# Windowed attention and two float64-weight feed-forward layers on one core: the sign of the weights carried by ScalarE's parametric ReLU, and the order of the work found anew

## The chip, the cores and the metric

The kernel runs on one core of one Trainium2 chip. The metric is the device time of one execution in microseconds (us), as the median of several runs. A profiled execution shows where that time goes: TensorE (PE, with its weight loads as PEld), VectorE (DVE), ScalarE (ACT), GpSimd (POOL) and the DMA queue that SyncE (SP) issues.

## The reference, cut to what matters

Attention over 4 batches, 8 heads, 576 positions and head size 64 (heads 0 to 3 see the last 32 positions, heads 4 to 7 every fourth of the last 128) gives x of 2304 x 512. Two feed-forward layers follow:

```python
def _moe_ref(x, w_in, w_out) -> np.ndarray:       # w_in 512 x 2048, w_out 2048 x 512
    h = x @ w_in
    g = h * np.cos(h)
    return (g @ w_out).astype(np.float32)
...
def _moe2_ref(x, w_gate, w_val, w_out) -> np.ndarray:   # 512 x 1536 twice, 1536 x 512
    gate = 1.0 / (1.0 + np.exp(-(x @ w_gate)))
    val = x @ w_val
    return (gate * val @ w_out).astype(np.float32)
...
        out['moe_' + k] = m[k]
```

The five weight matrices are float64 (a float32 draw times a Python float scale). The chip reads each as pairs of 32-bit words, and the kernel makes float32 values of them itself.

## The kernel before, in words

**The work.** Attention is done in units of 192 positions and half of the heads. The first layer goes over six chunks of 384 tokens. It takes 96 steps: `mlp_tasks(n)` multiplies one chunk with one block of 128 columns of w_in (`mm_h`, 12 matmuls into `ps_h`), makes h * cos(h) on ACT and DVE (`turn`, `part`, `cosine`, `g`, `g_hi`, `g_lo`) and multiplies with one block of w_out (`mm_x2`, 12 matmuls into four `acc` tiles). Steps 0 to 47 use the first eight column blocks for all six chunks, and the attention of later chunks runs beside them. Steps 48 to 95 use the other eight blocks. At the end of a chunk's eight steps, `take` (in `x2_out`) empties the four `acc` tiles, in the second half by an addition on DVE; the next chunk's first `mm_x2` needs those banks. The second layer follows, with pairs of chunks and seven products in place of eight.

**The weights.** 68 of the weight tiles of 128 x 512 values go through `w_tasks(i)`. Each is loaded as words (`raw`, printed as `wst`: the even words are the low halves of the doubles, the odd words the high halves). `low` (ACT) moves the low words down by 29 bits. `mag` reads the high word as a float32 and multiplies by 2^-112, which corrects the exponent; it stands on ACT, or on DVE where the scheduler finds DVE free first (`alt`). `shift` (DVE) moves the result up by three bits, which pushes the sign out. `top` (DVE) puts the sign back by taking the top bit of the high word. `rnd` (DVE) adds the low words. `hi` and `lo` split the value into two parts for TensorE, `lo` and the like on POOL.

**The order.** Nothing is ordered by hand. `Plan` is a scheduler that runs while the kernel is built: every task has an engine, a duration in a table, predecessors, buffers that it takes and gives back, and a priority. The task names are those of `add(("w_mag", i), ...)`. The priority is a place in the program plus a number by name from `NUDGE`, for priorities under `NUDGE_UNTIL`. Every instruction of every engine's queue and of SP's comes out in the order that this run gives. A task with `port=True` is kept apart in the plan from others that use the same port. Where PE would be idle in the plan before step 7, `keep_warm` fills in matmuls of a 128 x 128 identity (`identb`); their number comes from the plan.

Of the kernel before, what the change touches and what calls it, by code (L numbers as in the profile page):

```python
# [9 lines left out]
F32 = mybir.dt.float32  # L10
# [4 lines left out]
AF = mybir.ActivationFunctionType  # L15
ALU = mybir.AluOpType
# [20 lines left out]
X2_LAG = 3.5  # L37
SEC = 2.75
W_PRIO, W_START = 4.5, -4
W_GATE = (12.0, 1.8, 36.0, 1.4, 70.0, 1.6)  # L40
W_PRE = (6.0, 1.3)
W_MIX = (2, 2)
PRE = (0, 2, 4, 6)
O_START, O_PACE, O_LEAD = 2.5, 1.05, 2.0
XS_LEAD = (15.0, 0.6)
QK_LEAD, V_LEAD = 2, 3.0
A_LEAD, EXP_LEAD = 2.1875, 0.5
COLD, DENSE = 1.25, 1.0
NUDGE_UNTIL = 16
NUDGE = {"head": 4.5, "k_out": 0.75, "load_qk": -0.75, "load_v": 3.75, "p_out": -2, "p_transp": -2.5, "pv": -3.75,  # L50
         "q_out": -0.5, "s_eps": 2.75, "s_exp": 1, "s_max": -1, "s_norm": -1.25, "s_rec": 3.5, "scores": -4.5, "transp": -0.25,
         "w_hi": -0.25, "w_load": 0.5, "w_mag": 2, "w_rnd": -0.5, "x": -10.25, "x_hi": -3.75, "x_save": -8.5}
WARM, WARM_NS = 1200, 57


class Plan:
# [28 lines left out]
    def add(self, key, eng, dur, fn, deps=(), prio=0.0, take=(), give=(), table=None, port=False, lat=None, step=None,  # L85
            after=(), gate=None, alt=None, dma=0):
        assert key not in self.tasks, key
        if prio < NUDGE_UNTIL:
            prio += NUDGE.get(key[0], 0.0)
        self.tasks[key] = dict(key=key, eng=eng, dur=dur, fn=fn, deps=deps, prio=prio, take=take, give=give, table=table,  # L90
                               port=port, lat=lat or 0, step=step, after=after, gate=gate, alt=alt, dma=dma)

# [136 lines left out]
def windowed_attention_mlp_kernel(ctx, tc, q, k, v, w_in, w_out, w_gate, w_val, w_out2, out):  # L229
# [12 lines left out]
    PE, ACT, DVE, POOL, SP = nc.tensor, nc.scalar, nc.vector, nc.gpsimd, nc.sync  # L242
# [20 lines left out]
    scale = 1.0 / float(D) ** 0.5  # L263
# [41 lines left out]
    late = {}  # L305
# [12 lines left out]
    add = plan.add  # L318
# [48 lines left out]
    def pos(g):  # L367

        if g < 0:
            return NEG_GS * g  # L370
        c = min(int(g / GPC), NC - 1)
        return begin[c] + (g / GPC - c) * FIRST[c]
# [19 lines left out]
    def w_tasks(i):  # L392
        key = kind, f = wseq[i]
        st = {}
        j = i - 2 * F1
        if i in w_pre:
            need = W_PRE[0] + (w_order.index(i) - 2 * CUT) * W_PRE[1] + 14
        elif i < 2 * CUT:
# [3 lines left out]
        elif kind == "out2":  # L402
            need = W_GATE[4] + (j - 2 * F2) * W_GATE[5] + 8
        else:
            need = NSTEP + SEC * f
        pr = need - W_PRIO + i * 1e-3
        pre = 0 <= j < 2 * F2 and f in PRE
        block = j >= 0 and not pre
        second = kind == "val" or kind == "out2" and f % 2 == 1
        wid = (kind == "out2", f // 2 if kind == "out2" else f)  # L410
        nw = j // 2
# [10 lines left out]
            t = st["raw"][:, :, 0]  # L422
            ACT.activation(out=t, in_=t.bitcast(U32), func=AF.Copy, scale=2.0**-29)  # L423

        def mag(on_dve=False):

            st["c"] = wst.tile([P, DM], I32, tag="wc", name="wc")
            c, x = st["c"].bitcast(F32), st["raw"][:, :, 1].bitcast(F32)
            if on_dve:
                DVE.tensor_scalar(c, x, 2.0**-112, None, op0=ALU.mult)  # L430
            else:
                ACT.activation(out=c, in_=x, func=AF.Copy, scale=2.0**-112)

        def shift():
            DVE.tensor_scalar(st["c"], st["c"], 3, None, op0=ALU.logical_shift_left)

        def top():
            DVE.scalar_tensor_tensor(st["c"], st["raw"][:, :, 1], -0x80000000, st["c"], op0=ALU.bitwise_and,
                                     op1=ALU.bitwise_or)

        def rnd():
            to = st["c"]
# [18 lines left out]
        elif j < 0 or pre:  # L461
            gate = W_PRE[0] + (w_order.index(i) - 2 * CUT) * W_PRE[1]
        else:
            gate = need - 8 if kind == "out2" else min(W_GATE[2] + j * W_GATE[3], need - 8)
        add(("w_load", i), "sp", 550, load, [], pr - 2 if i >= 2 * FIRST[0] else max(NEG_GS * (i / 4 - 6) + W_START, pos(-A_LEAD - 1) - QK_LEAD + 0.1), take=["raw"], dma=1900, gate=gate,
            after=[("w_load", w_order[w_order.index(i) - 1])] if i else [])
        add(("w_low", i), "act", 520, low, [("w_load", i)], pr)

        def keep():
# [3 lines left out]
        def again():  # L473
            SP.dma_start(out=lf(TB_AT[nw % 2], 2 * DM), in_=wf2[PRE.index(f)])

        add(("w_mag", i), "act", 550, mag, [("w_load", i)], pr, take=["wc"], alt=("dve", 335, lambda: mag(True), True))
        add(("w_shift", i), "dve", 335, shift, [("w_mag", i)], pr, port=True)
        add(("w_top", i), "dve", 600, top, [("w_shift", i)], pr, port=True)
        give = ["raw"] + (["wc"] if block else [])
        deps = [("w_top", i), ("w_low", i)] + (["late"] if block else []) + ([] if not block else [("w_rnd", i - 1)] if second else [("w_free", nw - 2)] if nw >= 2 else [])  # L480
        add(("w_rnd", i), "dve", 600, rnd, deps, pr, give=give, port=True)
        if pre:
            add(("w_keep", i), "sp", 450, keep, [("w_rnd", i)], pr, give=["wc"], dma=800)
            if second:
                pr = NSTEP + SEC * f - W_PRIO + i * 1e-3
                add(("w_again", nw), "sp", 450, again, [("w_keep", i - 1), ("w_keep", i), "late"] + ([("w_free", nw - 2)] if nw >= 2 else []),
                    pr - 2, dma=1200, gate=min(W_GATE[2] + j * W_GATE[3], NSTEP + SEC * f - 8))
                block_tasks(i, nw, wid, pr, [("w_again", nw)])
# [449 lines left out]
    def p2(n):  # L938
        return NSTEP + SEC * n

    def xs_tasks(s):
# [7 lines left out]
        for kk in range(2):  # L949
# [20 lines left out]

            base = p2(s * F2) - XS_LEAD[0] + kk * 7 * XS_LEAD[1]
            gate = base - 1.0
# [19 lines left out]
            for i, nm in enumerate(("a0", "s2", "a1", "s3", "s1", "b1", "s4")):  # L992
                pr = base + i * XS_LEAD[1]
                deps = src[nm] + [("x2", early, KD - 1)]
# [7 lines left out]
    def xs_wide(s, ca, cb):  # L1002
# [19 lines left out]

        base = p2(s * F2) - XS_LEAD[0]
        free = w_saved if s == 1 else [("o_save", s - 2, nm, i) for nm in ("A0", "A1", "B0", "B1") for i in range(TT)]
# [372 lines left out]
```

## Time and profile before

| | |
|---|---|
| median of 3 runs | 936.86 us (934.87 to 937.38) |
| profiled execution | 940.28 us, of which its span, first to last instruction, is 938.5 us |
| PE busy | 922.5 us, 98% of the span |
| DVE busy | 721.5 us, 77% |
| ACT busy | 491.4 us, 52% |
| POOL busy | 190.3 us, 20% |
| granted TensorE clock, mean | 0.994 |

A matmul is counted as busy from its start to its modelled end, so a busy PE can still start its matmuls at a larger distance than it could. Busy shares are means over stages that differ.

### The profile page before, as it was taken

The page shows a single profiled execution, that of the slowest core. Times are in us where ns is not written, and L with a number is a line of the kernel's source. Part 1 is how long each engine was busy: PE and PEld are TensorE (multiplying, and loading weights), DVE is VectorE, ACT ScalarE, POOL GpSimd, SP SyncE. Part 2 cuts the span into 40 slices and gives each one's busy share as a digit, 9 for nine tenths or more (in the row PEclk, how much of TensorE's full clock was granted, in tenths as well). Part 3 has the DMA queues.
Part 4 walks back from the last instruction along what each step waited for, and adds up shares of the span by engine and source line. Part 5 has one row for each costly group of instructions (what it writes and reads, how often), then busy time and mean ns, then how long its engine had stood idle before and what let it go on. Part 6 is the DMA issues. An engine that isn't in the chain of part 4 may idle for free.

```text
span 938.5 us, 19283 instructions
## 1 busy us (share of the span) xinstructions
PE 922.5 (98%) x6921; PEld 897.6 (96%) x6921; DVE 721.5 (77%) x1726; ACT 491.4 (52%) x1182; POOL 190.3 (20%) x208
## 2 busy tenths in 40 slices
PE   8999999999999999999989999999999999999998
PEld 7898989989999999999989999999999999999998
DVE  5898898878977878898989865775666786566683
ACT  5787868767776655555556622342333343332261
POOL 4444322232313444323242400000000000000000
PEclk9999999999999999999989999999999999999999
DMA  7976757576335799879877698877888987887693
GB/s 190 210 219 164 209 163 217 148 220 173 95 116 184 249 357 312 308 246 301 307 244 276 221 378 278 302 233 252 267 269 268 324 297 251 267 267 214 191 324 107
DMA packets 162639, 225.67 MB, mean 240 GB/s; under 512 B 60784, under 2 KB 127088, under 8 KB 161520
## 3 DMA queue, kind: packets, MB, share of 16 engines
q1 hardware_dynamic: 161744, 224.24, 74.6%
q8 instruction: 55, 0.90, 0.4%
q14 instruction: 40, 0.33, 0.1%
q10 hardware_dynamic: 800, 0.20, 0.1%
HBM read 168.82 MB, written 55.57 MB: 239 GB/s over the span
## 4 chain that ended last, share of the span: by engine, by line
PE 74%; DVE 11%; DMA 9%; issue 3%; ACT 3%; SPq 0%; ACTq 0%; DVEq 0%
PE acc L775 5%; PE ps_h L775 5%; PE ps_h L777 4%; PE ps_h L776 4%; PE acc L777 4%; PE acc L776 4%; PE ps_y L1082 4%; PE ps_y L1084 4%; PE ps_y L1083 4%; PE xy L1230 3%; DMA wst<-in_moe_w_out_dram 3%; PE xy L1232 3%; PE xy L1231 3%; PE ps_x L1082 3%; PE ps_x L1084 3%
## 5 line engine op out<-in xcount | busy, mean ns | idle before, releaser
L520 POOL TENSOR_TENSOR lr<-lf,lr 128x512 fp32r<-128x512 f32 (+1 forms) x72 | 92.1, 1297 | 170.1 <-ACT lr L516 137.0
L775 PE MATMUL acc<-gs,arena 128*128 128x384 f32 x240 | 85.0, 354 | 0.4 <-ACT o L911 0.3
L777 PE MATMUL acc<-gs,arena 128*128 128x384 f32 x240 | 80.7, 336 | 0.0
L776 PE MATMUL acc<-gs,arena 128*128 128x384 f32 x240 | 80.5, 335 | 0.0
L845 DVE TENSOR_TENSOR gs<-u,gs 128x384 fp32r<-128x384 f32 x96 | 68.5, 715 | 11.8 <-ACT gs L842 11.4
L1082 PE MATMUL ps_y<-arena 128*128 128x384 f32 x216 | 73.1, 338 | 0.2 <-DVE u L1100 0.2
L1084 PE MATMUL ps_y<-arena 128*128 128x384 f32 x216 | 72.4, 335 | 0.0
L1083 PE MATMUL ps_y<-arena 128*128 128x384 f32 x216 | 72.3, 335 | 0.0
L825 ACT ACTIVATE r<-ps_h 128x384 int32<-128x384 f32 x96 | 46.7, 486 | 48.7 <-PE ps_h L777 48.1
L832 ACT ACTIVATE u<-u 128x384 f32<-128x384 f32 x96 | 50.0, 523 | 39.3 <-DVE u L829 38.3
L775 PE MATMUL ps_h<-arena 128*128 128x384 f32 x192 | 68.6, 357 | 0.6 <-DVE arena L718 0.6
L835 DVE TENSOR_TENSOR u<-ps_h,u 128x384 f32<-128x384 f32 x96 | 52.8, 552 | 17.0 <-ACT u L832 16.4
L777 PE MATMUL ps_h<-arena,wb 128*128 128x384 f32 x192 | 65.1, 339 | 0.0
L776 PE MATMUL ps_h<-arena,wb 128*128 128x384 f32 x192 | 65.1, 339 | 0.0
L775 PE MATMUL ps_h<-arena,wb 128*128 128x384 f32 x192 | 65.1, 339 | 0.0
L777 PE MATMUL ps_h<-arena 128*128 128x384 f32 x192 | 64.5, 336 | 0.0
L776 PE MATMUL ps_h<-arena 128*128 128x384 f32 x192 | 64.4, 335 | 0.0
L829 DVE SCALAR_TENSOR_TENSOR u<-ps_h,r 128x384 f32<-128x384 f32 x96 | 52.9, 551 | 13.7 <-ACT r L825 13.4
L1115 ACT ACTIVATE sg<-sg 128x384 f32<-128x384 f32 x36 | 19.0, 527 | 83.7 <-DVE sg L1111 83.7
L674 ACT ACTIVATE s<-s,mx 128x80 f32<-128x80 f32 (+1 forms) x168 | 59.3, 358 | 0.1
L423 ACT ACTIVATE wst<-wst 128x512 int32<-128x512 uint32 x68 | 45.5, 672 | 24.0 <-DMA wst<-in_moe_w_in_dram 10.5
L775 PE MATMUL acc<-gs,wb 128*128 128x384 f32 x144 | 49.3, 343 | 4.2 <-DVE o L905 3.2
(201 smaller groups left out, 2948.3 us busy)
## 6 DMA issues: line engine op xcount, KB each, us to landing
arena<-wd SPq DMA_DIRECT2D x108, 512.0 KB, 4.7
lr<-od SPq DMA_DIRECT2D x42, 512.0 KB, 4.8
wd<-lr SPq DMA_DIRECT2D x36, 512.0 KB, 4.8
wst<-in_moe_w_out_dram SPq DMA_DIRECT2D x28, 512.0 KB, 4.7
arena<-od SPq DMA_DIRECT2D x21, 512.0 KB, 6.1
arena<-wd SPq DMA_DIRECT2D x36, 256.0 KB, 3.9
od<-lr SPq DMA_DIRECT2D x18, 512.0 KB, 4.7
wst<-in_moe_w_in_dram SPq DMA_DIRECT2D x16, 512.0 KB, 5.5
```

The lines of the kernel that those rows point to most:

```text
L520: POOL.tensor_tensor(out=l, in0=x, in1=h.bitcast(F32), op=ALU.subtract)
L674: ACT.activation(out=s, in_=s, func=AF.Exp, scale=-1.0, bias=row("mx", u)[:, i:i + 1], accum_out=row("rs", u)[:, i:i + 1])
L775: PE.matmul(ps, wh, xl, start=first, stop=False)
L776: PE.matmul(ps, wl, xh, start=False, stop=False)
L777: PE.matmul(ps, wh, xh, start=False, stop=last)
L829: DVE.scalar_tensor_tensor(st["u"], st["h"], INV_2PI, st["r"], op0=ALU.mult, op1=ALU.subtract)
L832: ACT.activation(out=st["u"], in_=st["u"], func=AF.Sin, scale=TWO_PI, bias=HALF_PI)
L835: DVE.tensor_tensor(out=st["u"], in0=st["h"], in1=st["u"], op=ALU.mult)
L845: DVE.tensor_tensor(out=st["gs"][:, 1, :], in0=st["u"], in1=st["gs"][:, 0, :].bitcast(F32), op=ALU.subtract)
L1082: PE.matmul(st[to], wh, xl, start=first, stop=False, **more)
L1083: PE.matmul(st[to], wl, xh, start=False, stop=False, **more)
L1084: PE.matmul(st[to], wh, xh, start=False, stop=kk == 1, **more)
```

## The change

`mag` uses the activation function Prelu in place of Copy, with the same factor 2^-112 and the slope 2^32 for negative values. A negative value so comes out with an exponent field that is larger by 32, and `shift` by three bits moves exactly that bit into the place of the sign, while the old sign bit falls out at the top. `top` is then not needed, and `rnd` waits for `shift`. `mag` stands on ACT alone; the form on DVE is gone. The numbers that set the order are others: four of the pacing constants change, `NUDGE` has new numbers, and two more tables, `NUDGE_MID` and `NUDGE_LATE`, reach the tasks with larger priorities, which had no such numbers.

```diff
-W_GATE = (12.0, 1.8, 36.0, 1.4, 70.0, 1.6)
-W_PRE = (6.0, 1.3)
+W_GATE = (13.0, 1.8, 36.0, 1.2, 70.0, 1.6)
+W_PRE = (6.0, 1.38)
...
-O_START, O_PACE, O_LEAD = 2.5, 1.05, 2.0
-XS_LEAD = (15.0, 0.6)
-QK_LEAD, V_LEAD = 2, 3.0
+O_START, O_PACE, O_LEAD = 2.2, 1.05, 1.2
+XS_LEAD = (15.0, 0.7)
+QK_LEAD, V_LEAD = 2.3, 3.0
...
-NUDGE_UNTIL = 16
-NUDGE = {"head": 4.5, "k_out": 0.75, "load_qk": -0.75, "load_v": 3.75, "p_out": -2, "p_transp": -2.5, "pv": -3.75,
...
+NUDGE_UNTIL, NUDGE_FROM = 16, 44
+NUDGE = {"k_out": -1.25, "load_qk": 0.5, "load_v": 2.5, "p_out": -4.5, "pv": -3.75, "s_eps": 2.25, "s_exp": 1,
...
+NUDGE_LATE = {"o_hi": -3.5, "o_lo": -3, "o_sum": -7.5, "w2": -0.25, "w2_save": -3.5, "w_again": 8.25, "w_blo": -2.75,
...
-        if prio < NUDGE_UNTIL:
-            prio += NUDGE.get(key[0], 0.0)
+        if key[0] != "warm":
+            prio += (NUDGE if prio < NUDGE_UNTIL else NUDGE_MID if prio < NUDGE_FROM else NUDGE_LATE).get(key[0], 0.0)
...
-        def mag(on_dve=False):
+        def mag():
 
             st["c"] = wst.tile([P, DM], I32, tag="wc", name="wc")
-            c, x = st["c"].bitcast(F32), st["raw"][:, :, 1].bitcast(F32)
-            if on_dve:
-                DVE.tensor_scalar(c, x, 2.0**-112, None, op0=ALU.mult)
-            else:
-                ACT.activation(out=c, in_=x, func=AF.Copy, scale=2.0**-112)
+            ACT.activation(out=st["c"].bitcast(F32), in_=st["raw"][:, :, 1].bitcast(F32), func=AF.Prelu, scale=2.0**-112,
+                           alpha=2.0**32)
 
         def shift():
             DVE.tensor_scalar(st["c"], st["c"], 3, None, op0=ALU.logical_shift_left)
 
-        def top():
-            DVE.scalar_tensor_tensor(st["c"], st["raw"][:, :, 1], -0x80000000, st["c"], op0=ALU.bitwise_and,
-                                     op1=ALU.bitwise_or)
-
...
-        add(("w_mag", i), "act", 550, mag, [("w_load", i)], pr, take=["wc"], alt=("dve", 335, lambda: mag(True), True))
+        add(("w_mag", i), "act", 550, mag, [("w_load", i)], pr, take=["wc"])
         add(("w_shift", i), "dve", 335, shift, [("w_mag", i)], pr, port=True)
-        add(("w_top", i), "dve", 600, top, [("w_shift", i)], pr, port=True)
...
-        deps = [("w_top", i), ("w_low", i)] + (["late"] if block else []) + ([] if not block else [("w_rnd", i - 1)] if second else [("w_free", nw - 2)] if nw >= 2 else [])
+        deps = [("w_shift", i), ("w_low", i)] + (["late"] if block else []) + ([] if not block else [("w_rnd", i - 1)] if second else [("w_free", nw - 2)] if nw >= 2 else [])
```

The line numbers of the changed kernel are larger by six up to `low` and smaller by two from the block tasks on; between them `mag` is `L434` (`L432`), `shift` is `L438` (`L435`; the `L438` of before is `top`), `rnd` is `L445` (`L446`) and `hi` on ACT is `L452` (`L453`).

In the whole program as built, PE has the same matmuls but for the fillers: 267 on `identb` before, 286 now. DVE has 1728 instructions before and 1633 now, ACT 1018 and 1045; 34 of the 68 `mag` stood on ACT before, 68 do now. In the first 48 steps of the first layer 18 `mag` stood on ACT and 44 do now. PE's matmuls of scores and of values (`ps_s`, `ps_v`) stand in 54 unbroken groups before and in 51 now. Loads of an activation table: 21 before, 21 now.

**ACT at the start of the program.** `qbp` and `ktp` are the copies of the first transposed q and k (`ps_t`) that the first attention scores wait for, `wst` and `wc` are the weight tiles (`low`, `mag`), `s,rs` the exponentials. Before:

```order
L642 ACT_TABLE_LOAD
L642 ACTIVATE qbp<-ps_t 128x192
L423 ACTIVATE wst<-wst 128x512
L642 ACTIVATE ktp<-ps_t 128x192
L423 ACTIVATE wst<-wst 128x512
L432 ACTIVATE wc<-wst 128x512
L674 ACTIVATE s,rs<-s,mx 128x96 x2
```

Now:

```order
L640 ACT_TABLE_LOAD
L640 ACTIVATE ktp<-ps_t 128x192
L434 ACTIVATE wc<-wst 128x512
L429 ACTIVATE wst<-wst 128x512
L434 ACTIVATE wc<-wst 128x512
L452 ACTIVATE arena<-wc 128x512
L672 ACTIVATE s,rs<-s,mx 128x96 x2
```

Before, the second copy on ACT stood behind a weight tile; now the one copy that ACT makes stands ahead of all weights.

**DVE at the start of the program**, the first rows behind the clearing of buffers. Before:

```order
L646 COPY ktp<-ps_t 128x192
L430 TENSOR_SCALAR wc<-wst 128x512
L646 COPY qbp<-ps_t 128x192
L435 TENSOR_SCALAR wc<-wc 128x512
L438 SCALAR_TENSOR_TENSOR wc<-wst,wc 128x512
```

Now:

```order
L644 COPY qbp<-ps_t 128x192
L644 COPY ktp<-ps_t 128x192
L644 COPY qbp<-ps_t 128x192
L438 TENSOR_SCALAR wc<-wc 128x512
L445 ISA wc<-wst,wc 128x1024
```

Three of the four copies stand on DVE now, all ahead of the first weight work.

**DVE where the chunk of steps 72 to 79 hands its four `acc` tiles to the chunk of steps 80 to 87**, in the second half of the first layer. The additions that empty the tiles are `lf<-acc` and `o<-acc`; the row `u<-ps_h,r` at the top is `part` of step 82, `u<-ps_h,u` is `g`, `gs<-u,gs` is `g_lo`, `ISA lf<-wst,wc` is `rnd`, `arena<-xt,arena` and `xt<-xt` prepare the second layer. Before:

```order
L829 SCALAR_TENSOR_TENSOR u<-ps_h,r 128x384
L905 TENSOR_TENSOR lf<-acc_6127,lf 128x384
L905 TENSOR_TENSOR lf<-acc_6134,lf 128x384
L835 TENSOR_TENSOR u<-ps_h,u 128x384
L845 TENSOR_TENSOR gs<-u,gs 128x384
L446 ISA lf<-wst,wc 128x1024
L966 TENSOR_TENSOR arena<-xt,arena 128x384
L905 TENSOR_TENSOR o<-acc_6140,o 128x384
L829 SCALAR_TENSOR_TENSOR u<-ps_h,r 128x384
L905 TENSOR_TENSOR o<-acc_6146,o 128x384
```

Now:

```order
L903 TENSOR_TENSOR lf<-acc_6114,lf 128x384
L827 SCALAR_TENSOR_TENSOR u<-ps_h,r 128x384
L903 TENSOR_TENSOR lf<-acc_6120,lf 128x384
L903 TENSOR_TENSOR o<-acc_6129,o 128x384
L833 TENSOR_TENSOR u<-ps_h,u 128x384
L843 TENSOR_TENSOR gs<-u,gs 128x384
L903 TENSOR_TENSOR o<-acc_6138,o 128x384
L957 TENSOR_TENSOR xt<-xt 128x384
L438 TENSOR_SCALAR wc<-wc 128x512
```

The `rnd` and the `arena<-xt` row that stood between the second and the third addition are gone from there; three additions stand ahead of `g`. On PE, the new chunk's first twelve matmuls into `acc` were mixed with those into `ps_h` before and stand together now.

## Rows read from the trace of the kernel before

**Rows 1.** Page, busy time, share of the span and instructions of each engine.

```profile
PE 922.5 (98%) x6921; PEld 897.6 (96%) x6921; DVE 721.5 (77%) x1726; ACT 491.4 (52%) x1182; POOL 190.3 (20%) x208
```

**Rows 2.** Windows: length; PE, PEld, DVE, ACT, POOL busy (count); clock, DMA share, GB/s.

```profile
34.00:300.00 266.00, 262.77 (x2539) 244.56 (x2538) 223.17 (x687) 198.63 (x546) 87.17 (x103) 1.00 0.61 174
100.00:125.00 25.00, 24.62 (x239) 22.70 (x238) 20.67 (x70) 22.28 (x73) 8.38 (x11) 1.00 0.58 154
300.00:465.00 165.00, 164.45 (x947) 164.13 (x946) 143.71 (x259) 93.54 (x188) 60.75 (x48) 1.00 0.85 297
465.00:485.00 20.00, 16.33 (x78) 15.69 (x77) 17.17 (x30) 10.76 (x23) 5.83 (x5) 0.83 0.77 274
```

**Rows 3.** Waits of PE: waiter, releaser, us in total, times, longest.

```profile
PE acc L775 <- DVE o L905: 3.2, 1, 3.2
PE ps_s L655 <- ACT ktp L642: 1.8, 1, 1.8
```

**Rows 4.** Timeline of PE around that wait: start, us, instruction, idle before.

```profile
471.23 0.34 PE L777 MATMUL ps_h<-arena,wb 128*128 128x384 f32 x1
474.79 0.69 PE L775 MATMUL acc<-gs,wb 128*128 128x384 f32 x1 [3.22 <-DVE o L905]
475.27 0.52 PE L776 MATMUL acc<-gs,wb 128*128 128x384 f32 x1
475.60 0.52 PE L777 MATMUL acc<-gs,wb 128*128 128x384 f32 x1
```

**Rows 5.** Timelines of DVE and POOL in the same stretch, and one `rnd` before it.

```profile
462.20 0.69 DVE L446 CUSTOM_DVE_ANT_0 lf<-wst,wc 128x1024 uint16<-128x1024 uint16 x1
...
470.97 1.76 DVE L446 CUSTOM_DVE_ANT_0 lf<-wst,wc 128x1024 uint16<-128x1024 uint16 x1
472.66 1.61 DVE L966 TENSOR_TENSOR arena<-xt,arena 128x384 fp32r<-128x384 f32 x1
474.19 0.54 DVE L905 TENSOR_TENSOR o<-acc,o 128x384 f32<-128x384 f32 x1
...
470.76 4.09 POOL L520 TENSOR_TENSOR lr<-lf,lr 128x512 fp32r<-128x512 f32 x3 [3.60 <-ACT lr L516]
```

**Rows 6.** Timeline of all engines near the start, from 6.8 us.

```profile
6.81 0.71 PE L655 MATMUL ps_s<-ktp,qbp 64*64 64x96 f32 x12
8.21 0.67 ACT L423 ACTIVATE wst<-wst 128x512 int32<-128x512 uint32 x1 [2.40 <-DMA wst<-in_moe_w_in_dram]
8.94 0.33 ACT L642 ACTIVATE ktp<-ps_t 128x192 f32<-128x192 f32 x1
```

**Rows 7.** Groups by line and form: count, busy us, mean ns, idle before.

```profile
L438 DVE SCALAR_TENSOR_TENSOR wc<-wst,wc 128x512 int32<-128x512 int32 x68 | 51.3, 754 | 0.4
L430 DVE TENSOR_SCALAR wc<-wst 128x512 f32<-128x512 f32 x34 | 18.0, 529 | 9.4 <-DMA wst<-in_moe_w_in_dram 4.8 <-DMA wst<-in_moe_w_gate_dram 2.2 <-DMA wst<-in_moe_w_val_dram 1.7
L432 ACT ACTIVATE wc<-wst 128x512 f32<-128x512 f32 x34 | 22.6, 663 | 0.5 <-POOL arena L457 0.5
L516 ACT ACTIVATE lr<-lf 128x512 fp32r<-128x512 f32 x54 | 33.0, 626 | 13.4 <-DVE lf L508 6.8 <-DVE lf L446 2.9 <-issue 2.1
L832 ACT ACT_TABLE_LOAD x10 | 12.8, 1283 | 0.2
```

**Rows 8.** Timeline of PE: a group of attention matmuls between two of the layer's.

```profile
196.04 0.34 PE L777 MATMUL acc<-gs,arena 128*128 128x384 f32 x1
196.31 0.92 PE L702 MATMUL ps_v<-pt,vpl 96*64 96x64 f32 x24
197.16 0.44 PE L775 MATMUL acc<-gs,arena 128*128 128x384 f32 x1
197.44 0.34 PE L776 MATMUL acc<-gs,arena 128*128 128x384 f32 x1
```

**Rows 9.** Timeline of PE: fillers near the start.

```profile
14.02 1.50 PE L1345 MATMUL acc<-identb 128*128 128x128 bf16 x24
```

**Rows 10.** Waits of ACT on PE's products: waiter, releaser, us in total, times, longest.

```profile
ACT r L825 <- PE ps_h L777: 48.1, 48, 2.5
```

More of the change, by code (lines that the diff above doesn't have):

```diff
@@ L39 @@
 W_PRIO, W_START = 4.5, -4
-W_GATE = (12.0, 1.8, 36.0, 1.4, 70.0, 1.6)
-W_PRE = (6.0, 1.3)
+W_GATE = (13.0, 1.8, 36.0, 1.2, 70.0, 1.6)
+W_PRE = (6.0, 1.38)
 W_MIX = (2, 2)
 PRE = (0, 2, 4, 6)
-O_START, O_PACE, O_LEAD = 2.5, 1.05, 2.0
-XS_LEAD = (15.0, 0.6)
-QK_LEAD, V_LEAD = 2, 3.0
+O_START, O_PACE, O_LEAD = 2.2, 1.05, 1.2
+XS_LEAD = (15.0, 0.7)
+QK_LEAD, V_LEAD = 2.3, 3.0
 A_LEAD, EXP_LEAD = 2.1875, 0.5
 COLD, DENSE = 1.25, 1.0
-NUDGE_UNTIL = 16
-NUDGE = {"head": 4.5, "k_out": 0.75, "load_qk": -0.75, "load_v": 3.75, "p_out": -2, "p_transp": -2.5, "pv": -3.75,
-         "q_out": -0.5, "s_eps": 2.75, "s_exp": 1, "s_max": -1, "s_norm": -1.25, "s_rec": 3.5, "scores": -4.5, "transp": -0.25,
-         "w_hi": -0.25, "w_load": 0.5, "w_mag": 2, "w_rnd": -0.5, "x": -10.25, "x_hi": -3.75, "x_save": -8.5}
+NUDGE_UNTIL, NUDGE_FROM = 16, 44
+NUDGE = {"k_out": -1.25, "load_qk": 0.5, "load_v": 2.5, "p_out": -4.5, "pv": -3.75, "s_eps": 2.25, "s_exp": 1,
+         "s_move": -0.25, "s_norm": -0.25, "scores": -3.75, "transp": -0.25, "w": 6.5, "w_load": 1.25, "w_mag": -1, "w_rnd":
+         -4.75, "w_shift": -6, "w_top": -1.25, "x": -11.25, "x_hi": -2.5, "x_save": 5.25}
+NUDGE_MID = {"head": 1.5, "load_qk": -1.25, "p_out": -4.75, "pv": -2.25, "s_eps": -5.25, "s_exp": -1, "s_max": 0.25,
+             "s_move": -2.5, "s_rec": -0.5, "scores": 0.5, "transp": -3.5, "w": -0.25, "w_keep": 3.75, "w_load": -0.25, "w_shift":
+             -2, "w_top": 1.5}
+NUDGE_LATE = {"o_hi": -3.5, "o_lo": -3, "o_sum": -7.5, "w2": -0.25, "w2_save": -3.5, "w_again": 8.25, "w_blo": -2.75,
+              "w_low": -2.25, "w_mag": 3, "w_rnd": -5.75, "w_sum": 4.5, "w_top": -1.5, "x2": 0.25, "x2_save": -2.25, "x2_take":
+              -8.5, "x_again": 4.75, "xs": 5.75, "xs_hi": 1, "xs_load": -1.75}
 WARM, WARM_NS = 1200, 57
```

## Prediction

> **What bounds the kernel now.** I read the busy shares first, then windows over the stages, then the waits of PE, then the timelines of the few places where PE waits. PE is busy for 98% of the span and DVE for 77% [rows 1], so what DVE and ACT save counts only where PE waits for them. The windows show where that is. From 34 to 300 us, where attention runs beside the first half of the layer, PE is busy for 262.77 of 266 us; it is idle for 3.2 us in all, though DVE is busy for 223.17 us (84%) and ACT for 198.63 us (75%). From 300 to 465 us it starts 947 matmuls in 165 us, one every 0.174 us. From 465 to 485 us it starts only 78 in 20 us, at a granted clock of 0.83 [rows 2]. At 0.174 us these 78 take 13.6 us: 6.4 us are lost there, more than at any other place of the span. The waits of PE name it: 3.2 us for an addition on DVE that empties an `acc` tile; the next in size is 1.8 us at the start, for ACT's copy of `ktp` [rows 3]. The reader is to see that the kernel holds only some 20 us of slack: PE's 16 us without work [rows 1], the matmuls at the low clock, and the fillers.
>
> The large wait is this. PE starts a matmul at 471.23 us and the next at 474.79 us; the ones behind it stand 0.33 us apart (475.27, 475.60), about twice 0.174, so the clock has gone from its 2.4 GHz level to the one of 1.2 GHz for a while [rows 4]. The addition that PE waits for starts at 474.19 us on DVE. Ahead of it on DVE stand a `rnd` of 1.76 us, which takes 0.69 us at 462.20, and an `arena<-xt` of 1.61 us. In the same time POOL runs three subtractions without a gap, from 470.76 to 474.85 us [rows 5]. DVE's two instructions are late because POOL works, and the addition is late because it stands behind them.
>
> **The change part by part.** *DVE.* `top` goes away: 68 instructions of 0.754 us, 51.3 us of DVE. The 34 `mag` on DVE go too, 18.0 us [rows 7]. DVE's load falls from 721.5 us to about 652 us (before other tasks move). Taken alone this is worth nothing for the end: PE covers it nearly everywhere, and it counts through the two waits above.
>
> *ACT.* 34 `mag` come to ACT. The trace has no Prelu. The nearest row is the Copy in the same line, with the same tile and stride, 0.663 us; the bounds are 0.626 us, the Copy of `lr` of the same size, and 0.754 us, the slowest elementwise pass over such a weight tile, `top` on DVE [rows 7]. I take 0.663 us, as only the function differs: 34 x 0.663 = 22.5 us more, or 21 to 26 us. For all 68 the bounds make 43 to 51 us where 45 us are taken. ACT goes from 491 to about 514 us of the span. By the order, 26 of the 34 fall into the first 48 steps (44 `mag` on ACT there, 18 before), 17.2 us: ACT in the stretch of 34 to 300 us goes from 75% to at most 81%. Behind a Prelu in ACT's queue stand the copies and cosines that PE needs later, but ACT itself waits for PE's `ps_h` 48 times and 48.1 us in all [rows 10]. ACT is mostly ahead of PE, and this covers the added passes; I take 0, and price the other case below.
>
> *The start.* The second copy on ACT, `ktp`, ran at 8.94 us because it stood behind `low` of the first weight tile, which began only when the weights had landed, at 8.21 us. The scores in front had begun at 6.81 and taken 0.71 us [rows 6]. In the new order no copy stands behind weights: ACT makes one copy first, DVE the other three in a row. The 1.8 us of [rows 3] should go: -1.8 us, at the least 0 if another operand is late.
>
> *Fillers.* 286 instead of 267. Twenty-four took 1.50 us, so one stands for 0.06 us [rows 9]: 19 x 0.06 = +1.1 us.
>
> *Kinds of matmuls.* The layer's matmuls, the two kinds of attention matmuls and the transposes alternate less. In the order, groups of score and value matmuls number 51 instead of 54. Such a group costs at its entry 0.27 us where 0.174 is usual, and behind it the second matmul comes 0.28 us after the first [rows 8]: 0.2 us, or 0.3 us with what the last of the group may take longer. 3 x 0.3 = -0.9 us; between 0 and -2 us, as joined groups save a little elsewhere.
>
> *The handing over at step 80.* In the new order `rnd` and `arena<-xt` no longer stand between the additions, and the third addition follows the second directly. Only `g` and `g_lo` of one step stand ahead of the fourth. With that, POOL's subtractions have nothing to delay in front of the second and third tile. Of the 6.4 us I leave 0.4 us for a short wait for the first tile: -6.0 us; the bounds are -6.4 and 0. What is late next, if anything, is the fourth addition, behind `g_lo`, which needs ACT: twelve matmuls of `ps_h` and nine of `acc` stand ahead of its use on PE, 21 x 0.174 = 3.7 us, against five short instructions.
>
> *The other numbers of the order.* The second layer's tasks now have numbers of their own. PE is hardly ever idle there in the trace, so there is little to gain; whether a new place waits can't be read from the order. I take 0.
>
> Sum: -1.8 + 1.1 - 0.9 - 6.0 = -7.6 us on the profiled execution's 940.28 us (its span of 938.5 and 1.8 us around it): 932.7 us. The runs' median, 936.86 us, is 3.4 us lower. If those 3.4 us are part of the waits that go, only 4.2 us are left to gain in the runs and 932.7 us is their time too; if not, it is 936.86 - 7.6 = 929.3 us. I take the middle, **931.0 us**.
>
> **A rule against the change.** ACT loads a table when its function is not in the set that is active; one load is 1.283 us, and there were ten of them for the cosines [rows 7]. The built program has 21 loads before and after, with Prelu standing among exponentials and among cosines, so by the rows Prelu brings none. If it lacked a place in those sets, a load there and one back would go with nearly every one of 68: that is rival 3. The Trainium skill, "ScalarE: Activation LUTs", section "Table sets: the hidden batching unit", says that functions come in named sets, that cheap ones (relu, copy, identity and abs are its examples) lie in every set, and that work is to be batched by set; Prelu isn't among the examples. By that page's estimate of 2.66 us for a switch, 136 switches would add 362 us of ACT. The order's unchanged count speaks against it.
>
> **The rivals.**
> 1. *PE covers it, and the waits only move.* The order is a new draw: `shift`, `rnd` and the POOL subtractions are as many as before, and a row like the one of 1.76 us [rows 5] can stand ahead of another addition. Then only -1.8 + 1.1 - 0.9 = -1.6 us remain: 935.3 us. For it: the plan that was drawn up before had this wait as well. Against it: the additions stand closer in the new order.
> 2. *ACT becomes what PE waits for, in the attention stage: slower.* At 100 to 125 us ACT is busy for 22.28 of 25 us already [rows 2]. If each of the 26 added passes delays a copy or cosine that PE is waiting for by its own length, 26 x 0.663 = +17.2 us; with the sum, 931.0 + 17.2 = 948 us. It is slower than before from nine such passes on (5.9 us / 0.663), and by over 0.3% from thirteen to fourteen on. Against it: ACT's own waits for PE [rows 10].
> 3. *Prelu switches tables.* 68 x 2 x 1.283 = 174 us more on ACT, of it 44 x 2.57 = 113 us in the first 48 steps. ACT had 198.63 of 266 us there; with 17 and 113 us it needs 329 us, so some 63 us more: about 994 us.
> 4. *The small waits of the attention stage go as well*, since DVE falls there from 84%: another 3.2 us [rows 2], 927.8 us.
>
> **How the numbers follow.** The forecast 0.56, its own range 928 to 934 us. Rival 1 0.18, rival 2 0.11 (from a part of the passes, 940 to 948 us), rival 3 0.02, rival 4 0.13. The range of 924 to 939 us leaves out rivals 2 and 3 and a gain beyond rival 4 by more than the bounds of the parts (-6.4 for -6.0, -2 for -0.9). A difference under 0.3% (2.8 us) can't be told from none here; the limits are 934.05 and 939.67 us. Faster: 0.56 + 0.13 and a quarter of rival 1, 0.73. Same: the rest of rival 1 and a little of rival 2, 0.15. Slower: 0.12.
>
> **What would show it.** In the new profile: DVE's busy time near 652 us and ACT's near 514 us, with one Prelu at 0.63 to 0.75 us; no wait of PE for `ktp` near 7 us; 300 to 500 us with a matmul every 0.174 us throughout and a granted clock of 1.00; no more than 21 table loads. The prediction is wrong if PE has a new wait of over 2 us with a fall of the clock behind it, or if the waits of PE name ACT in the stretch to 300 us for more than 4 us in sum.

## The result and the profile after

The changed kernel takes 926.49 us (median of 4 runs, 925.78 to 928.57); the kernel before took 937.12 us in the same session (4 runs). The ratio is 0.9894, with a 95% interval of 0.987 to 0.9918. The forecast was 931.0 us, with a range of 924 to 939 us. The profiled execution of the changed kernel took 926.18 us, its span 924.4 us; that of before had a span of 938.5 us.

Busy times on the page of the changed kernel, to be read against [rows 1]:

```profile
PE 915.3 (99%) x6940; PEld 894.9 (97%) x6940; DVE 665.9 (72%) x1631; ACT 508.3 (55%) x1209; POOL 184.7 (20%) x208
```

Its windows, with the columns of [rows 2]; the first, to 34 us, was 29.17 us of PE at a clock of 0.95 before:

```profile
0.00:34.00 34.00, 29.80 (x466) 26.54 (x468) 22.93 (x118) 22.38 (x83) 16.43 (x38) 1.00 0.87 202
34.00:300.00 266.00, 265.26 (x2562) 249.82 (x2559) 202.78 (x647) 210.17 (x565) 83.73 (x105) 1.00 0.63 182
300.00:465.00 165.00, 165.00 (x951) 165.00 (x950) 129.80 (x239) 106.82 (x214) 68.68 (x54) 1.00 0.88 315
465.00:485.00 20.00, 20.00 (x117) 20.00 (x117) 18.55 (x37) 13.85 (x30) 5.00 (x4) 1.00 0.90 312
```

All waits of PE that the view lists for the changed kernel, with the columns of [rows 3]:

```profile
PE acc L1343 <- DVE identb L346: 1.6, 1, 1.6
PE ps_t L623 <- DMA q<-in_q_dram: 1.2, 3, 0.7
PE ps_t L623 <- PE ps_p L687: 0.8, 1, 0.8
PE ps_h L773 <- DVE arena L716: 0.7, 2, 0.5
PE ps_y L1080 <- DVE u L1098: 0.7, 1, 0.7
PE xy L1228 <- DVE lf L1297: 0.4, 1, 0.4
PE ps_t L623 <- DMA k<-in_k_dram: 0.3, 1, 0.3
```

The reader is to see three things. The stretch of 465 to 485 us has 117 matmuls where it had 78, at full clock. Between 34 and 300 us PE is idle for 0.7 us where it was for 3.2 us. Neither of the two waits of [rows 3] is left, and no wait is for ACT.

At the handing over at step 80, on DVE, the four additions (L903) of the changed kernel (in the form of [rows 5]):

```profile
459.31 0.56 DVE L903 TENSOR_TENSOR lf<-acc,lf 128x384 f32<-128x384 f32 x1 [0.86 <-PE acc L775]
459.78 0.55 DVE L827 SCALAR_TENSOR_TENSOR u<-ps_h,r 128x384 f32<-128x384 f32 x1
460.25 0.55 DVE L903 TENSOR_TENSOR lf<-acc,lf 128x384 f32<-128x384 f32 x1
460.71 0.55 DVE L903 TENSOR_TENSOR o<-acc,o 128x384 f32<-128x384 f32 x1
461.18 0.55 DVE L833 TENSOR_TENSOR u<-ps_h,u 128x384 f32<-128x384 f32 x1
461.64 0.55 DVE L843 TENSOR_TENSOR gs<-u,gs 128x384 fp32r<-128x384 f32 x1
462.11 0.55 DVE L903 TENSOR_TENSOR o<-acc,o 128x384 f32<-128x384 f32 x1
```

DVE now waits for PE here (0.86 us) and not PE for DVE.

Where the time went, by the starts of the steps' first `ps_h` matmuls in the profiled executions (us; the last rows are experiments from below):

| | to step 8 | 8 to 40 | 40 to 80 | 80 to 88 | 88 to the end | span |
|---|---|---|---|---|---|---|
| before | 91.8 | 195.1 | 167.6 | 40.1 | 443.9 | 938.5 |
| changed | 87.8 | 193.6 | 166.7 | 33.4 | 442.9 | 924.4 |
| difference | -4.0 | -1.5 | -0.9 | -6.7 | -1.0 | -14.1 |
| arith_only (E1) | 95.0 | 194.6 | 167.4 | 33.4 | 443.7 | 934.1 |
| numbers_only (E2) | 98.2 | 193.7 | 168.3 | 33.7 | 443.0 | 936.9 |
| hand_over (E5) | 90.3 | 195.0 | 167.6 | 34.6 | 443.5 | 931.0 |
| both_moves (E7) | 90.8 | 196.9 | 167.6 | 34.6 | 445.6 | 935.5 |
| arith_in_order (E8) | 90.9 | 196.1 | 166.7 | 39.4 | 443.3 | 936.4 |
| arith_moves (E9) | 89.6 | 198.6 | 166.7 | 33.3 | 443.6 | 931.8 |

The 14.1 us of the two profiles are 3.5 us more than the medians show: the profiled execution of before, at 940.28 us, had two falls of the clock, at the two waits of [rows 3]. In 35 runs of the kernel before on one chip the mean clock was 1.000 in 4, 0.998 in 17 and lower in 14; in the four of the changed kernel it was 0.999 or 1.000.

### The profile page after: what moved, and what is told of

It reads as the page before. It is cut to its first block, busy times and chain, and to the rows that moved or that the text cites. A ratio compares the mean times of both kernels' runs of the same rounds, so it can differ in the third digit from the quotient of the medians.

```text
span 924.4 us, 19266 instructions
## 1 busy us (share of the span) xinstructions
PE 915.3 (99%) x6940; PEld 894.9 (97%) x6940; DVE 665.9 (72%) x1631; ACT 508.3 (55%) x1209; POOL 184.7 (20%) x208
## 4 chain that ended last, share of the span: by engine, by line
PE 94%; DMA 4%; DVE 1%; ACT 1%; issue 0%; SPq 0%; DVEq 0%; ACTq 0%
PE ps_h L773 8%; PE acc L773 8%; PE acc L775 7%; PE acc L774 7%; PE ps_h L775 7%; PE ps_h L774 7%; PE ps_y L1080 4%; PE ps_y L1081 4%; PE ps_y L1082 4%; PE xy L1228 3%; PE xy L1230 3%; PE xy L1229 3%; PE ps_x L1080 3%; PE ps_x L1082 3%; PE ps_z L1080 3%; PE ps_z L1082 3%
## 5 line engine op out<-in xcount | busy, mean ns | idle before, releaser
L843 DVE TENSOR_TENSOR gs<-u,gs 128x384 fp32r<-128x384 f32 x96 | 64.4, 672 | 11.9 <-ACT gs L840 11.2
L1203 ACT ACTIVATE arena<-ub 128x384 fp32r<-128x384 f32 x62 | 31.0, 522 | 38.8 <-PE xy L1230 27.5
L434 ACT ACTIVATE wc<-wst 128x512 f32<-128x512 f32 x68 | 45.2, 667 | 6.7 <-DMA wst<-in_moe_w_in_dram 5.1
```

Source lines behind the costliest of these rows:

```text
L843: DVE.tensor_tensor(out=st["gs"][:, 1, :], in0=st["u"], in1=st["gs"][:, 0, :].bitcast(F32), op=ALU.subtract)
```

## The experiments

**Theory O**: the order decides; the gain comes from places where work that PE waits for stood behind slow or late work. **Theory D**: the time that DVE no longer spends decides. The rival in between: waits only move. Ratios are to the kernel before on the same chip, with 95% intervals; 0.001 is 0.94 us. A profile is one execution and can differ from the median by some us, so the text says which of the two a number comes from.

### The two halves apart, and the changed order with more work in it

E1 has the new arithmetic with the old numbers, E2 the new numbers with the old arithmetic; the plan then draws up an order of its own, with 370 and 375 fillers.

```diff
 # E1: diff of mag, shift, top and the deps as shown; NUDGE, W_GATE, ... unchanged
 # E2: NUDGE, NUDGE_MID, NUDGE_LATE, W_GATE, ... as shown; mag, top unchanged
```

> The new arithmetic alone: Prelu and no sign pass, with all numbers that set the order as before. The plan makes another order of it, with 370 fillers in place of 267 (before) and 286 (the change): 103 x 0.056 = 5.8 us more of them than before. Theory O (the gain lies in the order that the new numbers give; the freed VectorE time is only room for it): 937 + 5.8 less a part of the waits, 936 to 943 us. Theory D (VectorE's freed 69 us take the waits away by themselves, whatever the numbers): the 7 us of the attention stage and the 6 to 8 us of the handing over go, and only the fillers are lost: 937 - 14 + 6 = 927 to 931 us.

E1: 936.25 us, 0.9988 (0.9969 to 1.0007).

> The new numbers alone, with the sign pass and the two places for the magnitude as before. 375 fillers, 108 more than before: 6.0 us. Theory O in its simple form (the numbers are good by themselves): 926 to 933 us. Theory D: the load of VectorE is as before, so the waits are as well: 937 + 6 = 940 to 946 us. A third view (numbers and arithmetic only fit together): slower than before in this run and in the one with the arithmetic alone.

E2: 938.03 us, 1.0018 (0.9997 to 1.0038).

Neither half is faster; E1 lies in theory O's range, E2 in none of those named. In the profiles both lose the stall at step 80, E2 with `top` and all of DVE's old work in it: from step 80 to 88 they take 33.4 and 33.7 us. From step 8 to the end E1 takes 839.1 us and E2 838.7 us; the kernel before takes 846.7 us and the changed kernel 836.6 us. What they gain there they lose at the start: step 8 starts at 95.0 and 98.2 us, 3.2 and 6.4 us later than before, where the changed kernel has 87.8 us. The longest wait there for a product of another engine is 1.8 us in E1 (for `ktd` from ACT, 1.2 us in the kernel before) and 2.0 us in E2 (for `pt` from ACT), and 103 and 108 more fillers stand there than before. What is the fillers' part and what the waits' was not separated.

So by these profiles neither half needs the other to lose the stall; what only the two together have is a short start. As each plan is another draw, this doesn't say what each half is worth. The next two keep an order fixed.

E3 puts `top` back into the task of `shift`; E4 runs each Prelu twice. The order of all else is that of the changed kernel.

```diff
 # E3
         def shift():
             DVE.tensor_scalar(st["c"], st["c"], 3, None, op0=ALU.logical_shift_left)
+            DVE.scalar_tensor_tensor(st["c"], st["raw"][:, :, 1], -0x80000000, st["c"], op0=ALU.bitwise_and,
+                                     op1=ALU.bitwise_or)
 # E4
+            for _ in range(2):
                 ACT.activation(out=st["c"].bitcast(F32), ..., func=AF.Prelu, scale=2.0**-112, alpha=2.0**32)
```

> The changed kernel with the sign pass put back behind each shift, in the same task: the order of all other instructions stays as in the changed kernel, and VectorE gets 68 x 0.75 = 51 us more. Theory O: PE covers it but for a few places, 926 to 930 us. Theory D: waits of PE come back in the attention stage and at the handings over, as in the kernel before, 933 to 940 us.

E3: 951.73 us, 1.0161 (1.0127 to 1.0195): slower than before and than either theory expected, 25 us over the changed kernel for 51 us of DVE. Waits of PE and one window of E3:

```profile
PE acc L775 <- DVE o L909: 4.3, 3, 2.0
PE ps_h L775 <- DVE u L835: 3.7, 4, 2.5
```

```profile
300.00:465.00 165.00, 157.55 (x890) 155.65 (x889) 143.62 (x242) 95.03 (x193) 62.77 (x48) 0.99 0.81 289
```

PE starts 890 matmuls in 300 to 465 us and not 951, though DVE is no busier there (143.62 us) than it was before (143.71) [rows 2]. So the busy share alone is not what makes PE wait. The waits name the copies that empty the `acc` tiles in the first half (L909) and `g` (L835): this order leaves no room in front of them.

> The changed kernel with each Prelu made twice, the second over the first with the same result, in an unchanged order: ScalarE gets 68 x 0.667 = 45 us more, 44 x 0.667 = 29 us of it in the first 48 steps, where its share goes from 79% to 90%. If PE covers ScalarE's passes (the forecast's zero): 926 to 930 us. If ScalarE is what PE waits for (rival 2), up to 17 to 29 us more: 940 to 956 us.

E4: 933.21 us, 0.9966 (0.9951 to 0.9981), 6.7 us over the changed kernel for 45 us of ACT, between the two forecasts. Its attention stage:

```profile
34.00:300.00 266.00, 261.62 (x2554) 244.10 (x2555) 197.47 (x637) 227.75 (x603) 82.46 (x104) 1.00 0.61 176
```

ACT is busy there for 227.75 us (86%), and PE is idle for 4.4 us where it was for 0.7 us. No wait of PE names ACT here either; they name loads and products of DVE (`pt`, `mx`, `arena`). So ACT's cover is real, in this order it ends somewhere between a share of 79% and one of 86%, and a list of waits without ACT does not by itself show that ACT costs nothing.

### The places, one by one, in the order of the kernel before

For these the scheduler of the kernel before first writes its order down, and the instructions are then issued from that list, in which only the named tasks are moved (`behind(log, a, b)`: a directly behind b). Without a move the list gives the kernel before, row for row.

```diff
 # E5
+    behind(log, ("xs", 0, 0, "a0"), ("x2_take", 9, 3))
+    behind(log, ("w_rnd", 60), ("x2_take", 9, 3))
 # E6
+    behind(log, ("w_low", 0), ("k_out", 0, 1))
+    behind(log, ("w_mag", 0), ("q_out", 0, 1))
 # E7: all four.  E8: none, but every mag is a Prelu on ACT, and top is empty.  E9: all four, with E8's arithmetic.
```

> The kernel before, row for row, but on DVE the `rnd` of weight tile 60 and one `arena<-xt` stand behind the four additions that empty the `acc` tiles at step 80 and not between them. Theory O (the order: the stall at the handing over is what stands in front of the additions): the 78 matmuls in 465 to 485 us become about 114, the clock keeps its 2.4 GHz level there, and 6 to 6.5 us go: 930.5 us. Theory D (the time that DVE no longer spends is what counts, the wait is only one shape that its load takes): the two instructions delay something else, PE waits there instead, and the time stays within 2 us of 936.9 us.

E5: 936.84 us, 0.9965 (0.9946 to 0.9985): a gain of 3.3 us (1.4 to 5.1), half of what theory O expected. The window and DVE around the handing over:

```profile
465.00:485.00 20.00, 19.35 (x110) 18.59 (x109) 18.72 (x35) 12.90 (x28) 9.34 (x8) 1.00 0.78 285
```

```profile
469.56 0.55 DVE L905 TENSOR_TENSOR o<-acc,o 128x384 f32<-128x384 f32 x1
470.68 0.55 DVE L905 TENSOR_TENSOR o<-acc,o 128x384 f32<-128x384 f32 x1
471.14 1.45 DVE L446 CUSTOM_DVE_ANT_0 lf<-wst,wc 128x1024 uint16<-128x1024 uint16 x1
472.51 1.09 DVE L966 TENSOR_TENSOR arena<-xt,arena 128x384 fp32r<-128x384 f32 x1
```

`rnd` and `arena<-xt` are still slow (1.45 and 1.09 us), but PE waits for nothing behind them. The mechanism of the prediction is shown; by the profiles the place gives 5.5 us (40.1 to 34.6). What is missing to 6.4 us is partly the fall of the clock: with the wait still there, the window had a clock of 0.83 in the profile of before and 0.91 in those of E6 and E8, so 6.8 us at the lower level in the one case ((1 - 0.83) x 20 / 0.5) and 3.6 us in the others.

> The kernel before, row for row, but on ACT `low` of the first weight tile stands behind the copy of `ktp`, and on DVE `mag` of that tile behind the copy of `qbp`. The step of the prediction (the wait costs its own 1.8 us): 935.1 us. Against it, from the traces (behind that wait the clock falls to its 1.2 GHz level at 9.4 us for 3.4 us, in which half of the work is lost): 1.8 + 1.7 = 3.5 us go, 933.4 us, and no such fall is in the profile. If the wait only moves to another operand of the first scores: 936.9 us.

E6: 938.44 us, 0.9997 (0.998 to 1.0014): no gain that can be told, as in the third forecast. The wait for `ktp` is gone, and the clock is 1.00 to 34 us. Waits of PE for loads and another engine stand there instead:

```profile
PE ps_t L625 <- DMA q<-in_q_dram: 0.8, 2, 0.6
PE ps_p L689 <- DVE mx L667: 0.8, 1, 0.8
```

> Both moves in the kernel before: four instructions stand at other places, and the arithmetic with its `top` and all 69 us of DVE is kept. Theory O: the two gains add up, 6.4 + 3.5 us: 927.0 us, as fast as the changed kernel within 1 us. Theory D: without the freed DVE time not more than a third of it comes, 934 us or more.

E7: 935.68 us, 0.996 (0.9942 to 0.9977). Neither theory: the four moves give 3.8 us (2.2 to 5.4), about what E5 and E6 make when added up (3.3 and 0.3 us). The profile shows a third place that both E5's and E6's forecasts had left out. PE, and DVE, near 207 us in E7:

```profile
205.94 0.34 PE L777 MATMUL ps_h<-arena 128*128 128x384 f32 x1
208.24 1.76 PE L702 MATMUL ps_v<-pt,vdl 80*64 80x48 f32 x32 [1.97 <-issue]
```

```profile
207.07 0.43 DVE L430 TENSOR_SCALAR wc<-wst 128x512 f32<-128x512 f32 x1 [3.20 <-DMA wst<-in_moe_w_gate_dram]
207.41 0.23 DVE L667 CUSTOM_DVE_ANT_0 s<-ps_s,mp 128x80 f32<-128x80 f32 x1
```

The row of PE names "issue", so the cause has to be found from what ends just before 208.24. The `ps_v` tile comes from the same pool of banks as the scores. DVE's `s_max` (L667, eight passes from 207.41) reads the scores, and its fourth pass ends at 208.14 us; in the kernel before and in E5 `ps_v` starts 0.11 to 0.12 us behind that pass as well. `s_max` stood behind `mag` of a weight tile, and `mag` waited 3.20 us for the load. Behind the wait the clock fell (0.66 in 207 to 212 us). The same instructions in the kernel before, and in E6:

```profile
208.70 1.14 PE L702 MATMUL ps_v<-pt,vdl 80*64 80x48 f32 x32 [0.93 <-PE ps_h L777]
207.53 0.43 DVE L430 TENSOR_SCALAR wc<-wst 128x512 f32<-128x512 f32 x1 [2.17 <-DMA wst<-in_moe_w_gate_dram]
```

```profile
205.98 1.14 PE L702 MATMUL ps_v<-pt,vdl 80*64 80x48 f32 x32
204.71 0.43 DVE L430 TENSOR_SCALAR wc<-wst 128x512 f32<-128x512 f32 x1 [1.05 <-DMA wst<-in_moe_w_gate_dram]
```

| profile (us) | PE's last matmul before `ps_v` starts at | `mag` starts at | PE waits for |
|---|---|---|---|
| before | 207.43 | 207.53 | 0.93 |
| hand_over (E5) | 205.16 | 205.06 | 0.74 |
| start (E6) | 205.72 | 204.71 | none |
| both_moves (E7) | 205.94 | 207.07 | 1.97 |

The order at this place is the same in all four. Against the kernel before, PE comes 1.49 us earlier in E7 and `mag` only 0.46 us, so the wait grows. But in E5 and E6 PE comes even earlier than in E7, and `mag` starts 2.0 and 2.4 us earlier. So the wait is real and stands where a load can be late; that it grew because the other waits were taken away is not shown, and over the runs E7 loses nothing against the sum of E5 and E6. What sets the time at which the load lands was not tried.

> The new arithmetic in the order of the kernel before: each `mag` is a Prelu on ACT at the place that it had in the order, `top` is left out, and nothing else moves, so the number of fillers stays 267. DVE is freed of 69 us and ACT gets 22.5 us more. Theory O: the `low` that makes `ktp` wait and the `rnd` at the handing over stay where they are; what goes are small waits of the attention stage, at most the 3.2 us that PE is idle there: 934 to 937 us. Theory D: most of the gain comes with it, 928 to 931 us. Rival 2 of the prediction (ACT has no room at the places where DVE had the `mag`): over 937 us.

E8: 937.85 us, 0.999 (0.9972 to 1.0008), which is 0.9 us less than before on the same chip; on the 936.9 us of the forecasts that makes 936.0 us, in theory O's range. DVE is busy for 646.5 us up to 900 us of the span, where it was for 699.5 us; in a fixed order these 53 us, with ACT's added passes, change nothing that can be measured, and theory D falls for this order.

> The new arithmetic and the two moves, in the order of the kernel before; all else stands as it stood there, with its 267 fillers. By itself the arithmetic gave -0.1% in this order and the two moves -0.4%. If they only add up: 0.995 of the time before, about 933.5 us where before has 938. If the waits share a cause (with DVE's time freed the moved instructions delay nothing else, with the stalls gone the freed time counts): 0.990 to 0.992, 929 to 930.5 us, near the changed kernel. If most of the gain is the new order of the attention stage as a whole: no better than 0.994.

E9: 932.86 us, 0.9937 (0.9916 to 0.9958), a gain of 5.9 us (3.9 to 7.9). Adding up E7 and E8 makes 4.7 us, which lies in that interval. They don't reach the changed kernel, whose variants below took 0.9857 to 0.988 on the same chip. In the profile a place of the same kind as E7's stands out, in another unit of the attention, at 230 us. PE, ACT and DVE in E9:

```profile
230.19 0.34 PE L777 MATMUL ps_h<-arena 128*128 128x384 f32 x1
233.10 1.84 PE L702 MATMUL ps_v<-pt,vdl 80*64 80x48 f32 x32 [2.57 <-issue]
```

```profile
230.70 0.65 ACT L423 ACTIVATE wst<-wst 128x512 int32<-128x512 uint32 x1 [3.17 <-DMA wst<-in_moe_w_in_dram]
231.25 0.64 ACT L430 ACTIVATE wc<-wst 128x512 f32<-128x512 f32 x1
```

```profile
231.93 0.43 DVE L435 TENSOR_SCALAR wc<-wc 128x512 int32<-128x512 int32 x1 [3.81 <-ACT wc L430]
232.27 0.23 DVE L667 CUSTOM_DVE_ANT_0 s<-ps_s,mp 128x80 f32<-128x80 f32 x1
```

The chain is load, `low`, `mag`, `shift`, `s_max`, bank, `ps_v`. From step 24 to 32 E9 takes 53.7 us, the changed kernel 49.4: in these two executions this one wait with its fall of the clock (0.76 in 231 to 238 us) is 4.3 of the 7.4 us between the two spans. It is not so in every run: four of E9's six runs had a mean clock of 1.000, so no such fall, and took 930.16 to 933.42 us, still over every run of E10 to E12 on the same chip (at most 928.33 us).

### The changed kernel with one thing other

```diff
 # E10
-        if cold():
+        if cold() and i % 3 != 1:
 # E11, in the list of the changed kernel
+    behind(log, ("w_load", 1), ("load_qk", 1))
+    behind(log, ("w_mag", 1), ("s_exp", 0, 0, 0))
+    behind(log, ("w_shift", 1), ("k_out", 1, 1))
 # E12, in the same list
+    behind(log, ("k_out", 0, 1), ("w_shift", 0))
```

> The changed kernel with every third filler left out, the order of all else kept. The step of the prediction (a filler stands on the path and costs its 0.06 us): about 95 x 0.06 = 5.7 us less than the changed kernel, so 0.983 of before. Rival (the fillers fill time in which PE would wait for loads and copies anyway): the same time as the changed kernel, 0.989 to 0.990. Second rival (without them PE pauses, the granted clock falls to its 1.2 GHz level at the start and 2 to 4 us are lost): 0.991 to 0.994, with a fall in the profile.

E10: 927.05 us, 0.9864 (0.9846 to 0.9883), with 191 fillers. That is 0.003 or 2.8 us under the changed kernel's ratio, half of the 5.7 us and not the same time either; the intervals of the two overlap. Waits of PE and the window to 34 us:

```profile
PE ps_t L623 <- DMA q<-in_q_dram: 2.5, 4, 1.2
PE ps_t L623 <- DMA k<-in_k_dram: 1.8, 3, 1.4
```

```profile
0.00:34.00 34.00, 27.52 (x371) 23.50 (x372) 20.89 (x114) 21.05 (x76) 15.61 (x37) 0.90 0.82 190
```

The waits for loads are 4.3 us where they were 1.5 us, and the clock falls. In three of its five runs the mean clock was 0.996 (927.05 to 927.52 us); in the two with 1.000 the times were 923.85 and 924.97 us, under every run of the changed kernel. By the profile the fall costs up to 3.4 us ((1 - 0.90) x 34), and step 8 still starts at 88.0 us, as it does with all fillers (87.8). So fewer fillers seem to save about 3 us and to lose them again in the runs in which the clock falls.

> The changed kernel, but the load of the second weight tile stands behind the loads of the second unit's queries and keys on SP, and its `mag` and `shift` a few places later on ACT and DVE. PE's waits for these loads (1.2 us for queries, 0.3 us for keys) should go. If nothing else is late: 1 to 1.5 us less than the changed kernel, 0.988 of before; if the start is bounded by all loads together, the wait moves to the weights: no change against it, 0.989 to 0.990.

E11: 925.63 us, 0.9857 (0.9838 to 0.9876). The waits for queries are gone, those for keys are 1.4 us. Its interval overlaps with the one of the changed kernel, which was measured in another session; whether this version is faster is not settled.

> The changed kernel, but on DVE the copy of `ktp` stands behind `shift` of the first weight tile, so that the first scores wait for weights as in the kernel before. By the two profiles (a wait of 1.8 us, and a fall of the clock behind it that takes another 1.7 us): 3 to 4 us slower than the changed kernel, 0.993 of before. By the experiment that took this wait out of the kernel before (-0.03%, at most 0.2%): under 2 us, 0.989 to 0.991.

E12: 927.51 us, 0.988 (0.9864 to 0.9897). The wait for `ktp` is back, shorter, with another at 35 us, and the clock stays at 1.00:

```profile
PE ps_v L700 <- DVE pt L644: 1.6, 1, 1.6
PE ps_s L653 <- DVE ktp L644: 0.9, 1, 0.9
```

By the profile 2.1 us are lost (a span of 926.5 for 924.4 us), over the runs none that can be told. E6 had it so from the other side.

## Why the prediction was right, point by point

The time came out 4.5 us under the forecast and inside its range; the faster side held, and neither of the two signs against it came (the longest wait left is 1.6 us, at the start, and no wait names ACT). That the sum came so near is in part luck. In the old order the two places gave less over the runs than the forecast had: the handing over 3.3 us and not 6.0, the start 0.3 us and not 1.8. About 4 us came from the order of the rest, for which the sum had nothing. Step by step:

- **DVE, "taken alone this is worth nothing"**: right in the order of before (E8, -0.9 us with an interval from -2.6 to +0.8, with ACT's added passes in it). The new order can't do without it: E3, which puts `top` back, gives half of the 51 us to the end, by waits for `g` and for the copies that empty the `acc` tiles. Another order can lose the stall with `top` in it (E2).
- **DVE's busy time**: 665.9 us and not 652. The 69.3 us were summed from durations of rows that overlap: before, a `top` began at 468.04 us with 0.68 us, and the next instruction began at 468.65, so 0.07 us belong to both. By this one place, 102 x 0.07 = 7 us is an estimate of it; of the other 7, 3 are seven copies of `ktd` that moved from ACT to DVE (6 there before, 13 now), which is also a part of why ACT has 508.3 us and not 514. The rest stays open.
- **ACT, 0 us**: right within what PE is idle for, 0.7 us in 34 to 300 us, where ACT has 210.17 us, 79%, and at most 81% was foreseen. That no wait of PE names ACT says less, as none does in E4, which is slower. E4 shows how near the limit is. Rival 2 did not come.
- **A Prelu by the row of the Copy, no table load**: right; the rows are below.
- **The start, -1.8 us**: mis-sized. In the profile step 8 starts 4.0 us earlier, since a fall of the clock goes as well; over the runs E6 gives 0.3 us with an interval from a gain of 1.9 to a loss of 1.3. PE then waits there for loads (1.0 us) and for `mx` (0.8 us).
- **Fillers, +1.1 us**: the size is not settled. E10's 95 fewer give 2.8 us by the ratios, 0.03 us for one and not 0.06, with overlapping intervals; the waits for loads grow by 2.8 us where they are gone, and the clock falls in three runs of five.
- **Kinds of matmuls, -0.9 us**: not tried by itself; it stays open.
- **The handing over, -6.0 us**: right place and mechanism, mis-sized: 3.3 us over the runs (1.4 to 5.1), 5.5 us in the profiles. It was sized from one execution in which the clock fell for longer than in others. That POOL's work is what made `rnd` and `arena<-xt` late was not tried by a run; rows in the last section bear on it.
- **"The other numbers of the order", 0 us**: for the second layer, of which this step speaks, it holds: behind step 88 the two profiles differ by 1.0 us. But the numbers reach the attention stage too, and there the sum had no term. Rival 4 had it, whose 927.8 us are the nearest of the five times; of its 3.2 us of idle time in that stage 0.7 us are left. From step 8 to 40 the profiles of before and after differ by 1.5 us.

Together, over the runs: about 10 us, of which 5.9 us are the two moves and the arithmetic in the old order (E9). The other 4 us ((0.9937 - 0.9894) x 937, each of the two with 2 us of interval to either side) lie in the new order of the rest, and their cause stays open. E9's profile is behind the changed kernel's by 1.8 us to step 8 and by 5.0 us from 8 to 40, of which 4.3 us are `s_max` behind a weight tile that had not landed; but the fall of the clock in it is missing in four of six runs, and no run moved `s_max` alone.

## What to carry to other kernels

- Look for instructions that the bounding engine needs and that stand in a queue behind work on a tile that hasn't landed, or behind a pass that can be slow; here a maximum stood behind `mag` and an addition behind a slow `rnd`. How long such a place makes PE wait changed from execution to execution (none to 1.97 us at the same place in the same order), so one profile doesn't price it.
- Time saved on an engine that isn't the bound was worth nothing that could be measured in the old order, and the new order could not do without it; test both with the order held fixed.
- When a scheduler draws the order anew, compare by stages: E1 and E2 had gained 7.6 and 8.0 us behind step 8 by the profiles and lost them at the start, which the end-to-end time alone hides.
- Size a stall from several executions, or keep both ends: here the profiled execution of the kernel before was 3.4 us over its median run.

## What the runs showed of the hardware

Prelu with the factor 2^-112 and the slope 2^32 costs what Copy costs ([rows 7], 663 ns), and ACT's table loads are as many as before:

```profile
L434 ACT ACTIVATE wc<-wst 128x512 f32<-128x512 f32 x68 | 45.2, 667 | 6.7 <-DMA wst<-in_moe_w_in_dram 5.1 <-POOL arena L456 1.1 <-issue 0.2
L830 ACT ACT_TABLE_LOAD x10 | 12.8, 1283 | 0.2
L672 ACT ACT_TABLE_LOAD x9 | 11.5, 1283 | 0.2
```

So Prelu stands among exponentials and cosines at no price here. The Trainium skill, "ScalarE: Activation LUTs", section "Table sets: the hidden batching unit", says that cheap functions lie in every set; by the rows Prelu behaves like one of them.

A wait of PE and a fall of the clock don't go together by length alone. The wait for `ktp` was 1.8 us before with a fall behind it, and 2.0 us in E5 without one:

```profile
PE ps_s L655 <- ACT ktp L642: 2.0, 1, 2.0
```

```profile
6.00:14.00 8.00, 6.00 (x108) 5.49 (x107) 6.09 (x24) 4.64 (x17) 2.07 (x3) 1.00 0.72 159
```

In E8 it was 2.3 us, again without one. What decides it was not tried.

A `rnd` on DVE was slow where it began behind a subtraction of POOL that was already running, and not where it began first. Two `rnd` of the changed kernel, and POOL beside them:

```profile
396.42 0.69 DVE L445 CUSTOM_DVE_ANT_0 lf<-wst,wc 128x1024 uint16<-128x1024 uint16 x1
400.92 1.79 DVE L445 CUSTOM_DVE_ANT_0 lf<-wst,wc 128x1024 uint16<-128x1024 uint16 x1
```

```profile
396.44 1.84 POOL L518 TENSOR_TENSOR lr<-lf,lr 128x512 fp32r<-128x512 f32 x1 [2.69 <-ACT lr L514]
400.67 4.21 POOL L518 TENSOR_TENSOR lr<-lf,lr 128x512 fp32r<-128x512 f32 x3 [2.39 <-ACT lr L514]
```

In the profiles of before and after, nine `rnd` of this form began first and took 0.68 to 0.69 us, as they do with no POOL work beside. Eight began behind a running subtraction: seven took 0.85 to 1.79 us, and one, at the very end of it, 0.68 us. This is the reason that the prediction gave for the slow `rnd` at the handing over. The addition at 474.19 us ([rows 5]) also began in POOL's work and took 0.54 us; it reads an `acc` tile. No run changed POOL's place alone.
